# Attention and expert routing on one core: first keys in three parts, late small loads, pad rows spread over SyncE, a new order

## The chip, the core and the metric

One core of a Trainium2 chip runs the whole program. The engines are TensorE (PE), VectorE (DVE), ScalarE (ACT), GpSimd (POOL) and SyncE (SP), which only issues DMAs. Each works through its own instructions strictly in the order in which they stand; engines meet through semaphores. The metric is device microseconds of one launch.

## The reference, cut to what matters

Four batches of attention with pooled keys, then a top-1 mixture of eight experts over all 49,152 rows:

```python
kv_pool = kv.reshape(B, H // r, r, W // r, r, C).mean(axis=(2, 4))   # 4 x 4 means: 768 keys of 128
k = v = kv_pool.reshape(B, -1, C) @ w_sr
s = (q @ k.transpose(0, 2, 1)) / np.sqrt(C)
a = np.exp(s - s.max(-1, keepdims=True)); a /= a.sum(-1, keepdims=True) + 1e-09
x = (a @ v).reshape(B * S, D)                                         # 4 x 12288 rows of 128
logits = unit(x) @ unit(expert_emb).T / tau                           # eight experts
expert_idx = np.argmax(logits, axis=1); gate_w = softmax(logits)[expert_idx]
for e in range(E):
    out[mask] = gate_w[mask, None] * (np.maximum(x[mask] @ w1[e], 0.0) @ w2[e])   # hidden size 1024
```

## The kernel before

**Attention.** The queries are worked through in 96 steps of 512 (24 per batch), each in four tiles of 128 queries by 768 keys. A tile's scores S come from PE, DVE takes the row maxima `nm`, ACT the exponentials `p`. The first `ka` = 16 steps multiply q and K in f32 (`s_mm`, tile `kf`); in the later ones K and V are f16 pairs (a high part and a remainder), and S is a sum of f16 products. For the product with V, `p` is as a rule split into the f16 tiles `phi` and `plo`, turned by DMA transposes, and multiplied in three terms (line 926). In some half steps (two tiles), chosen by the string `em` of the table `X`, `p` stays f32: PE transposes it against `ident` (line 441) and multiplies it with `pw` as it is (line 917). These are called unsplit halves here.

**The head.** Before any score, the keys of the first batch must exist. Twelve loads of 512 KB (`kv_load_0`) bring kv in chunks; DVE adds neighbours in each (lines 501 and 505, tile `kvt`), PE sums rows and turns the chunk with the matrix `window` (line 513), ACT scales six chunks into `pT` (line 564), PE multiplies 384 columns with `w_sr` (line 517), and ACT or DVE copies them to `kf` (lines 578 and 580, letters `kc`). So K comes in two halves. The pooling of batches 1 to 3 is done later in the same way at line 467, on the engine named by the string `kd`.

**Experts.** Rows are sorted by expert through scatters by POOL into `xs_rows` in DRAM, in groups, while attention runs. Then each tile `t` takes 256 rows of one expert (`load`: a transposing DMA, line 1595, and a small one, 1596); 184 whole tiles come first and up to 23 remainder tiles of 128 rows last, with tile 176 the first that has to wait for the last group's scatter. `load_w` copies the expert's 1 MB of f16 weights into one of three buffers `wbuf`, under a condition on a register, since the copy is skipped when the expert stays the same. Row numbers reach SP by register loads (TENSOR_LOAD) from `off_i` and `wi_i`, with checks of their bounds (FUSED_REGOPS and an assert, line 1561). PE computes `ph` (line 1628) and `po` (line 1664). Padding behind each expert's last row is written by eight DMAs of `pad`, and 576 KB of padding rows by `dummies`.

**What sets the order.** Nothing is dispatched at run time. Every operation is put with `add(engine, duration, key, function, *deps)` into a `Plan`; a list scheduler with estimated durations, keys from the table `X` and stand-in delays (`slack`, `dma`) writes the program, so each engine's order is fixed by numbers. DVE and POOL share a port to the local memory; the plan keeps some of their work apart by the flag `port`. Writes into PE's banks go by turns: three tiles `s_tiles` for S, which the head uses too.

Of the kernel before, what the change touches and what calls it, by code (L numbers as in the profile page):

```python
# [44 lines left out]
X = dict(  # L45
    ka=16, da=8.159, di=14.892, db=12.933, dma=1.729, ahead=2.284, av=6.502, av0=1.846, lb=-4.518, l2=3.102, qt=1.955,
    lead=18.786, x=-14.465, r=0.691, s=-1.205, p=14.572, x0=3.032, r0=2.092, s0=1.377, p0=5.813, qt0=-0.263,
    pm="acabacbccabcccabbdacccb", pl="aaaaabaa", nm="AAADA", xn="DAAA", nm0="ADD", xn0="AA", we="ddcdcdaaadcdaccd",
    h=13.707, kv=20.916, kvs=2.272, w0=-14.405, start=23.312, early=21.36, wd=12.952, xw=1.718, qd=21, qs=21.178,
    ql=9.747, em="---------AA-A-A-A-AA-DM-", et=2.859, ec=-0.864, v0=123.118, sd=1, qu=1.461, q0=-66.525, avd=0.626,  # L50
    m=1.052, end=-3.563, ne=-4.766, ge=-0.689, kd="DPD", gk=547.052, wq="AADADDAD", kv1=10.617, kvs1=0.757, tg=-0.003,
    tl=0.397, qe="------------------------", gap=1.8, nb="ADDDD-DAAD-A---DDD-A--D-----DDD--A-D-A-D-DA----D",
    sqm="AASAAAAAAAAAPAAAPSSAPPPS", qm="AAADDDADDAADDADAAADAAAAD", xh="ADPPDADPDAADDAAPAADADADD", nl="-",
    slack={'ACT PE': 0.131, 'ACT DVE': 0.095, 'ACT POOL': -0.009, 'ACT ACT': -0.082, 'DVE PE': 0.32, 'DVE ACT': 0.274, 'DVE POOL': 0.348, 'DVE DVE': 0.013, 'PE ACT': 0.263, 'PE DVE': 0.071, 'PE POOL': -0.1, 'PE SP': -0.11, 'POOL ACT': 0.46015762370487345, 'POOL DVE': 0.111, 'POOL PE': 0.1, 'POOL POOL': 0.07},
    wt=4.0, leadr=22.0, wr=55.0, kf=16, kc="DA", kk=2.199, su=-1.199, vk=-5.844, om="AAAADADA", og=2.027,
# [4 lines left out]
def attention_moe(  # L60
# [71 lines left out]
    rows2 = [cpool.tile([P, GT, RP], F32, name=f"rows{i}") for i in range(2)]  # L132
    ident = cpool.tile([P, P], F32, name="ident")
# [70 lines left out]
    ctx.enter_context(tc.manual_schedule())  # L204
# [34 lines left out]
    class Op:  # L239


        def __init__(self, eng, dur, key, fn, deps, dma, take, free, hold, lands, port, stage):
            self.eng, self.dur, self.key, self.fn, self.dma = eng, dur, key, fn, dma
            self.port = port
            self.take, self.free, self.lands, self.stage = take, free, lands, stage
            self.left, self.users, self.ready, self.end = 0, [], 0.0, None
            if hold:
                self.ready = key + X["start"] - X["early"]
            for d in set(deps):
                if d is not None:  # L250
                    self.left += 1
                    d.users.append(self)

    class Plan:
# [36 lines left out]
        def run(self, begin):  # L291
# [23 lines left out]
            while any(count):  # L315
# [89 lines left out]
                for u in op.users:  # L405
                    if op.dma is not None and u.dma is not None and eng == u.eng and not op.lands:
                        ready = op.end
                    elif op.dma is not None:
                        ready = self.moved + X["dma"]
# [97 lines left out]
    def kv_t_0(i):  # L507
        v = st[0].pop(("kvt", i))
        a, j = divmod(i, NKC // 2)
        st[0]["pp", a] = s_tiles[a]  # L510
        for g in range(KC // R):
            k = (j * (KC // R) + g) * 32
            nc.tensor.matmul(s_tiles[a][:, k : k + 32], v[:, g, 0, :], window, start=True, stop=True)

    def kv_k_0(a):
        st[0]["kp"] = s_tiles[2].rearrange("p (a b) -> p a b", a=2)[:, :, :HB]
        nc.tensor.matmul(
            st[0]["kp"][:, a, :], wsr[:, :C], st[0]["pT"][:, a * HB : (a + 1) * HB], start=True, stop=True
        )

    def kv_max_0(a):
        if a == 0:
# [3 lines left out]
            out=m[:, a : a + 1], in_=st[0]["kp"][:, a, :], axis=AX.X, op=ALU.max, apply_absolute_value=True  # L526
# [33 lines left out]

    def kv_mean(b, a):
# [10 lines left out]
    def kv_k_copy(b, a):  # L572
        if a == 0:
            st[b]["kf"] = kvs.tile([P, NK], F32, tag="kf", name=f"kf{b}")
        if b == 0:
            out, x = st[0]["kf"][:, a * HB : (a + 1) * HB], st[0]["kp"][:, a, :]
            if X["kc"][a] == "A":
                nc.scalar.mul(out, x, SCALE)
            else:
                V.tensor_scalar(out=out, in0=x, scalar1=SCALE, scalar2=None, op0=ALU.mult)  # L580
            return
        nc.scalar.copy(out=st[b]["kf"][:, a * HB : (a + 1) * HB], in_=st[b].pop(("kp", a))[:, :HB])

# [214 lines left out]
    def s_mm(k, j):  # L798
        t = s_tiles[s_turn(k, j)]
        ks[k]["s", j] = t[:, :NK]  # L800
        if unscaled(k):
            for lo, hi in ((0, 512), (512, NK)):
# [737 lines left out]
    def pads():  # L1540
        rows = nc.values_load_multi_w_load_instructions(
            base_i[0:1, :], engines=[nc.sync.engine], min_val=0, max_val=(E - 1) * CAP + NT
        )[1]
        for e in range(E):
            o = nc.s_assert_within(rows[e], e * CAP, e * CAP + NT)
            ins = nc.sync.dma_start(out=xs[ds(o, TR), :].rearrange("(p j) c -> p j c", j=TR // P), in_=pad)
            for key in (*keys, "loads"):
                tc.declare_no_dep(ins.ins, group=key, reason="rows past an expert's last")
            tc.add_to_no_dep_group("loads", ins.ins)
# [6 lines left out]
    def value(name, src, t, top):  # L1556
# [177 lines left out]
    def kv_rows_0():  # L1734
# [3 lines left out]
        for i in range(NKC):  # L1738
            t0, tag = -70.0 + 0.1 * i, kv_tag(i)
            o = took(tag, add("SP", 0.45, t0, lambda i=i: kv_load_0(i), *turn(tag, KV_BUFS[tag]), dma=1.43))  # L1740
# [3 lines left out]
            if i == 3:  # L1744
                x_set = setup(X["su"], x_wsr, x_tau, x_emb, c)
# [5 lines left out]
    def kv_ops(b):  # L1751
# [18 lines left out]
        for a in range(2):  # L1770
            if b == 0:
                key = -60.0 + a
                m = add("ACT", 0.37, key, lambda a=a: kv_mean(b, a), turned[NKC // 2 * (a + 1) - 1], *(turn("pT", 1) if a == 0 else ()))
            else:
                key = t0 + 14.0 + a
                last = mine[(a + 1) * NQR // 2 - 1]
                o = add("PE", 0.64, key, lambda a=a: kv_t(b, a), last, *turn("pT", 1), take=f"pp{b}_{a}")
                reads("pooled", o)
                m = add(
                    "ACT", 0.37, key, lambda a=a: kv_mean(b, a), o, *(turn("pT", 1) if a == 0 else ()),  # L1780
                    free=f"pp{b}_{a}",
                )
# [3 lines left out]
            if b == 0:  # L1786
                o = add("PE", 0.8, key, lambda a=a: kv_k_0(a), m, x_wsr)
                if a == 0:
                    turn("s2", 1), turn("kf", 1)
                    took("s2", o)  # L1790
                else:
                    reads("s2", o)
                reads("pT", o)
                copies.append(add("DVE", 0.5, key + 0.5, lambda a=a: kv_max_0(a), o, *copies))
                on = ENG[X["kc"][a]]
                whole_k.append(add(on, 0.5, key, lambda a=a: kv_k_copy(0, a), o, *whole_k))
                if a == 0:
                    took("kf", whole_k[0])
                reads("s2", copies[-1], whole_k[-1])
                continue  # L1800
# [458 lines left out]
```

## Time and profile before

| | |
|---|---|
| time, three runs | 1948.08, 1948.6, 1950.21 us (median 1948.6) |
| profiled execution | 1957.1 us, of it 1955.4 us span |
| granted TensorE clock | 0.998 |
| PE | 1907.6 us busy, 98% of the span |
| DVE, ACT, POOL | 86%, 75%, 66% |

Busy time counts an engine's instructions, not its waiting. PE's matmuls are pipelined, so a row can begin before the last one ends. The head is the time before the first score, about 27 us; attention runs to about 1770 us with expert tiles woven in, and the rest is the last expert tiles.

### The profile page before, as it was taken

Reading aid. Unit: us, or ns where it says so; the run is one execution under the profiler, and the core shown is the slowest. Engines: PE = TensorE matmul, PEld = TensorE weight load, DVE = VectorE, ACT = ScalarE, POOL = GpSimd, SP = SyncE. Lnnn points to the kernel's source line nnn. Section 1 sums busy time; section 2 is a strip of 40 time slices with the busy share of each in tenths; the row PEclk is TensorE's granted clock in tenths of the full one; section 3 lists DMA queues with packets and bytes.
Section 4 is the critical chain, followed back from the end, with each engine's and each line's share of the span. In section 5 each row is a group of like instructions: output and inputs, shape, how many; then the busy total and the mean of one; then the engine's idle time right before and its main releaser. Section 6 shows DMA issues by size and latency. Waiting matters only on the chain. (4 is left out here: it accounts for less than half of the span.)

```text
span 1955.4 us, 63753 instructions
## 1 busy us (share of the span) xinstructions
PE 1907.6 (98%) x23536; PEld 1677.0 (86%) x23536; DVE 1674.3 (86%) x4037; ACT 1469.7 (75%) x3162; POOL 1292.3 (66%) x1857
## 2 busy tenths in 40 slices
PE   6999999999999999999999999999999999999988
PEld 4787788888888888888888888888888888898988
DVE  7899999988988879888989988988888898886645
ACT  4888877877788778877777877877877788764543
POOL 2547587678886777685676675766766865766544
PEclk9999999999999999999999999999999999999999
DMA  7998889989888999888989899887877777763443
GB/s 256 250 265 206 205 170 175 170 159 172 182 174 169 199 200 177 166 176 153 181 176 170 171 222 177 180 154 144 178 142 161 165 147 145 156 130 67 101 106 122
DMA packets 870923, 333.24 MB, mean 170 GB/s; under 512 B 825794, under 2 KB 836171, under 8 KB 868432
## 3 DMA queue, kind: packets, MB, share of 16 engines
q1 hardware_dynamic: 844624, 274.95, 71.9%
q0 software_dynamic: 24640, 53.53, 9.4%
q8 instruction: 186, 3.05, 0.7%
q14 instruction: 129, 1.06, 0.2%
q10 hardware_dynamic: 1344, 0.66, 0.1%
HBM read 271.41 MB, written 63.19 MB: 171 GB/s over the span
## 5 line engine op out<-in xcount | busy, mean ns | idle before, releaser
L1635 ACT ACTIVATE hh<-ph 128x512 f16<-128x512 f32 x754 | 447.7, 595 | 237.8 <-PE ph L1628 196.0
L1640 DVE SCALAR_TENSOR_TENSOR hl<-ph,hh 128x512 f16<-128x512 f32 x754 | 513.0, 683 | 108.9 <-ACT hh L1635 103.0
L1628 PE MATMUL ph<-x,wbuf 128*128 128x256 f16 x4416 | 594.0, 273 | 11.4 <-DMA wbuf<-w_prep 8.3
L207 POOL DMA_INDIRECT xs_rows<-rows,pi x384 | 442.7, 1153 | 176.6 <-issue 40.0
L207 POOL DMA_INDIRECT out_dram<-o,m x350 | 381.8, 1091 | 227.1 <-ACT o L1684 45.4
L1628 PEld LDWEIGHTS <-wbuf 128*128 128x128 f16 x4848 | 438.7, 98 | 79.1 <-DMA wbuf<-w_prep 12.1
L1664 PE MATMUL po<-wbuf,hh 128*128 128x128 f16 x6032 | 460.3, 219 | 2.9 <-DVE hl L1640 1.1
L1664 PEld LDWEIGHTS <-hh 128*128 128x128 f16 x6176 | 400.5, 98 | 20.7 <-issue 2.6
L810 PE MATMUL s<-k,qT 128*128 128x512 f16 (+1 forms) x1920 | 363.9, 326 | 1.4 <-DVE nm L821 1.4
L821 DVE CUSTOM_DVE_ANT_0 p<-s,scales,qa 128x768 f32<-128x768 f32 x320 | 323.3, 1010 | 41.9 <-PE s L810 38.7
L875 DVE SCALAR_TENSOR_TENSOR plo<-p,phi 128x768 f16<-128x768 f32 x358 | 349.1, 976 | 5.8 <-ACT phi L861 3.5
L840 ACT ACTIVATE p<-p,nm 128x768 f32<-128x768 f32 x320 | 298.8, 934 | 59.2 <-DVE nm L821 56.8
L926 PE MATMUL xp<-v,pthi 128*128 128x136 f16 (+1 forms) x4392 | 319.7, 223 | 1.4 <-ACT pT L564 0.8
L1664 PE MATMUL po<-wbuf,hl 128*128 128x128 f16 x3016 | 291.5, 219 | 0.0
L926 PEld LDWEIGHTS <-pthi 128*128 128x128 f16 x4392 | 278.8, 98 | 14.3 <-issue 2.0
L861 ACT ACTIVATE phi<-p 128x768 f16<-128x768 f32 x310 | 260.8, 843 | 6.6 <-DMA pthi<-phi 3.5
L810 PEld LDWEIGHTS <-qT 128*128 128x128 f16 x1920 | 178.3, 98 | 87.0 <-issue 1.8
L1664 PEld LDWEIGHTS <-hl 128*128 128x128 f16 x3088 | 205.0, 98 | 0.7
L926 PE MATMUL xp<-v,ptlo 128*128 128x136 f16 x2196 | 189.8, 223 | 2.6 <-DMA ptlo<-plo 2.6
L946 ACT ACTIVATE x<-xp,rn 128x135 f32<-128x135 f32 x304 | 96.5, 372 | 77.6 <-DVE rn L938 59.5
L960 POOL TENSOR_TENSOR rows<-x,rows 128x256 f16<-128x256 f32 x192 | 137.4, 720 | 19.1 <-ACT rows L956 14.2
L926 PEld LDWEIGHTS <-ptlo 128*128 128x128 f16 x2196 | 144.0, 98 | 3.0 <-DMA ptlo<-plo 3.0
(416 smaller groups left out, 2045.4 us busy)
## 6 DMA issues: line engine op xcount, KB each, us to landing
wbuf<-w_prep SPq DMA_DIRECT2D x202, 1026.0 KB
q<-in_q_dram SPq DMA_DIRECT2D x48, 512.0 KB
kvt<-in_kv_dram SPq DMA_DIRECT2D x24, 768.0 KB
wf<-in_moe_w_dram SPq DMA_DIRECT2D x16, 512.0 KB
kvt<-in_kv_dram SPq DMA_DIRECT2D x12, 512.0 KB
xs_rows<-rows,pi POOLq DMA_INDIRECT x384
out_dram<-o,m POOLq DMA_INDIRECT x350
w_prep<-wo SPq DMA_DIRECT2D x8, 514.0 KB
```

The costliest lines, as they stand in the source:

```text
L207: ins = nc.gpsimd.indirect_dma_start(out=dst, out_offset=bass.IndirectOffsetOnAxis(ap=idx, axis=0), in_=src, in_offset=None, bounds_check= ...
L810: nc.tensor.matmul(t[:, lo:hi], qs[:, l, :], r[:, lo:hi], start=i == 0, stop=i == 2)
L821: V.tensor_tensor_reduce(out=p, in0=ks[k].pop(("s", j)), in1=scales[:, 4:5].broadcast_to([P, NK]), scale=ks[k]["fac"], scalar=3.0e38, op0= ...
L840: nc.scalar.activation(out=p, in_=s, func=AF.Exp, bias=ks[k].pop(("nm", j)), scale=1.0 if unscaled(k) else -1.0)
L861: nc.scalar.mul(hi, p, PSC)
L875: V.scalar_tensor_tensor(out=lo, in0=ks[k].pop(("p", j)), scalar=PSC, in1=hi, op0=ALU.mult, op1=ALU.subtract)
L926: nc.tensor.matmul(ks[k]["xp", h][:, i, :e], l[:, c, :], r[:, c, :e], start=n == 0, stop=n == len(terms) - 1, skip_group_check=True,)
L960: nc.gpsimd.tensor_tensor(out=r[:, :, C : 2 * C], in0=ks[k]["x"][:, 2 * h : 2 * h + 2, 0:C], in1=r[:, :, 0:C], op=ALU.subtract)
L1628: nc.tensor.matmul(ph[:, kk * n : (kk + 1) * n], weights(t, o + f, P), r, start=i == 0, stop=i == 2)
L1635: nc.scalar.activation(out=hh, in_=ts[t]["ph", u], func=AF.Relu)
L1640: V.scalar_tensor_tensor(out=hl, in0=ts[t].pop(("ph", u)), scalar=0.0, in1=ts[t]["hh", u], op0=ALU.max, op1=ALU.subtract)
L1664: nc.tensor.matmul(ts[t]["po"][:, j * C : (j + 1) * C], h[:, kk * n + j * P : kk * n + (j + 1) * P], weights(t, f, P), start=u == 0 and i ...
```

## The change

**K in three parts.** The chunks 6 to 11 go to another bank, and `kv_mean_0`, `kv_k_0` and `kv_k_copy_0` run over the columns 0 to 384, 384 to 640 and 640 to 768. The first two tiles of S are split, so that their first 512 columns need only the first two parts.

```diff
+    KP = ((0, HB), (HB, NK - X["kt"] * 64), (NK - X["kt"] * 64, NK))
+    def kv_k_0(n):
+        a, (lo, hi) = min(n, 1), KP[n]
+        if n < 2:
+            st[0]["kp", a] = s_tiles[1][:, :HB] if a == 0 else s_tiles[2][:, 512 : 512 + HB]
         nc.tensor.matmul(
-            st[0]["kp"][:, a, :], wsr[:, :C], st[0]["pT"][:, a * HB : (a + 1) * HB], start=True, stop=True
+            st[0]["kp", a][:, lo - a * HB : hi - a * HB], wsr[:, :C], st[0]["pT"][:, lo:hi], start=True, stop=True
         )
...
+            if k == 0 and j < X["sh"]:
+                o = add("PE", 0.86, key, lambda j=j: s_mm(k, j, 0), hi, lo, *whole_k[:2], *turn(tag, 1))
+                uses["kf"][0].append(o)
+                o = add("PE", 0.43, key, lambda j=j: s_mm(k, j, 1), o, *deps)
```

**Small loads and constants.** The load of `tau` (one number to 128 partitions) and the padding rows of `dummies` move from about 0 and 33 us to later places. The constants are written before the plan's own work on their engines, and the chain that normalises `emb` (`setup`) follows the last chunk, not the fourth.

```diff
+    ctx.enter_context(tc.manual_schedule())
     ident = cpool.tile([P, P], F32, name="ident")
...
-    x_tau = add("ACT", 0.1, -60.0, lambda: nc.scalar.dma_start(out=tau_b, in_=tau.broadcast_to([P, 1])), dma=0.06)
+    x_tau = add("ACT", 0.3, X["tau"], lambda: nc.scalar.dma_start(out=tau_b, in_=tau.broadcast_to([P, 1])), dma=0.3, hold=True)
...
-    x_dummies = add("ACT", 0.1, 30.0, dummies, dma=3.1, hold=True)
+    x_dummies = add("ACT", 0.1, TS[NSTEP - 10], dummies, dma=4.2, hold=True)
...
-            if i == 3:
-                x_set = setup(X["su"], x_wsr, x_tau, x_emb, c)
+            if i == NKC - 1:
+                x_set = setup(X["su"], x_wsr, x_emb, c)
```

**Padding on SP, and checks.** The eight writes of `pad` become eight operations, each with its own register load, put 4 us apart in the plan. The register loads of the last tiles leave their bounds checks out.

```diff
-    def pads():
-        rows = nc.values_load_multi_w_load_instructions(
-            base_i[0:1, :], engines=[nc.sync.engine], min_val=0, max_val=(E - 1) * CAP + NT
-        )[1]
-        for e in range(E):
-            o = nc.s_assert_within(rows[e], e * CAP, e * CAP + NT)
...
+    def pads(e):
+        o = nc.sync.value_load(base_i[0:1, e : e + 1], min_val=e * CAP, max_val=e * CAP + NT)
...
-                src[0:1, i : min(i + 4, NTILE)], engines=[nc.sync.engine], min_val=0, max_val=top
+                src[0:1, i : min(i + 4, NTILE)], engines=[nc.sync.engine], min_val=0, max_val=top,
+                skip_runtime_bounds_check_because="the rows and weights of a tile are bounded where they are worked out",
```

**The table.** Most numbers and strings of `X` are new. Two lines of many:

```diff
-    ql=9.747, em="---------AA-A-A-A-AA-DM-", et=2.859, ec=-0.864, v0=123.118, sd=1, qu=1.461, q0=-66.525, avd=0.626,
-    m=1.052, end=-3.563, ne=-4.766, ge=-0.689, kd="DPD", gk=547.052, wq="AADADDAD", kv1=10.617, kvs1=0.757, tg=-0.003,
+    xw=1.718, qd=21, qs=19.803, ql=10.318, em="---A-----MA-D-M-A-AA-DM-", et=3.494, ec=0.254, v0=104.065, sd=1,
+    qu=-0.424, q0=-65.932, avd=-0.301, m=-0.039, end=-3.551, ne=-6.905, ge=-1.176, kd="DPP", gk=228.829,
```

In the program as written this makes 120 transposes of `p` on PE and 120 unsplit products with V in place of 108 each, 24 and 12 fewer split products of the two kinds at line 926, 182 pairs of DMA transposes in place of 183, and 16 pooling adds of each size on POOL in place of 8, since batch 3 is pooled there and not on DVE.

On PE, the head. Before: the columns of the last two chunks (`kvt` 10 and 11) into the bank s_159, the transposes of q, `emb` and `wsr`, the second half of K into s_160, and the first S tile.

```order
L513 MATMUL s_159<-window,kvt_10_232 128x32 x2
L513 MATMUL s_159<-window,kvt_11_242 128x32 x2
L441 MATMUL pq_285<-ident,q_251 128x128 x4
L441 MATMUL pe<-ident,emb_sb 128x8
L441 MATMUL pe<-ident,wsr 128x128
L517 MATMUL s_160<-pT_238,wsr 128x384
L1275 MATMUL pe<-wt 128x7
L803 MATMUL s_158<-kf_255,qT_294 128x512
```

The same place in the change:

```order
L515 MATMUL s_160<-window,kvt_10_221 128x32 x2
L523 MATMUL s_160<-pT_233,wsr 128x256
L515 MATMUL s_160<-window,kvt_11_227 128x32 x2
L443 MATMUL pq_274<-ident,q_235 128x128 x4
L523 MATMUL s_160<-pT_233,wsr 128x128
L818 MATMUL s_158<-kf_245,qT_286 128x512
L543 MATMUL bound<-m_250,ones_97 128x1 x2
L818 MATMUL s_158<-kf_245,qT_286 128x256
```

Behind the last chunk stand now a product of 128 columns and no work of `setup`; the first 512 columns of S stand ahead of the 256 others, with the product `bound` between.

On SP, near the end of attention. Before: the register loads, weight copies and the eight writes of `pad` (the rows between repeat the check and the write).

```order
L1571 DMA wbuf_2878<-w_prep 128x4104
L1541 TENSOR_LOAD base_i
L1541 ISA x16
L1545 REGISTER_ALU
L1545 ISA
L1546 ISA
L1546 DMA xs_rows<-pad 128x144
```

The same place in the change:

```order
L1583 DMA wbuf_2799<-w_prep 128x4104
L1556 TENSOR_LOAD base_i
L1556 ISA x2
L1557 ISA
L1557 DMA xs_rows<-pad 128x144
L1569 TENSOR_LOAD off_i
L1569 ISA x2
L1607 ISA
L1607 DMA_TRANSPOSE x_40967<-xs_rows 128x2x256
L1608 ISA
L1608 DMA ml<-xs_rows 128x2x2
L1556 TENSOR_LOAD base_i
```

One `pad` write stands there now between a weight copy and the load of a tile, and the other seven are spread in the same way from tile 170 to tile 176.

## Rows read from the trace of the kernel before

**Rows 1.** The page: busy time of each engine, share of the span, instructions.

```profile
PE 1907.6 (98%) x23536; PEld 1677.0 (86%) x23536; DVE 1674.3 (86%) x4037; ACT 1469.7 (75%) x3162; POOL 1292.3 (66%) x1857
```

**Rows 2.** Busy time by stage: us, PE, PEld, DVE, ACT, POOL, PEclk, DMA share, GB/s.

```profile
600.00:800.00 200.00, 196.03 (x2484) 172.92 (x2481) 174.63 (x421) 158.36 (x342) 149.44 (x218) 1.00 0.96 191
...
1000.00:1200.00 200.00, 195.34 (x2500) 172.81 (x2499) 178.55 (x427) 156.33 (x344) 134.02 (x195) 1.00 0.95 188
```

**Rows 3.** DMA queues between 5 and 7 us: packets, MB, share of 16 engines.

```profile
q1 hardware_dynamic: 66, 0.20, 28.3%
q10 hardware_dynamic: 133, 0.00, 3.5%
```

**Rows 4.** Timeline of the head: start, us, engine, line, operation, idle before.

```profile
4.66 0.69 DVE L501 TENSOR_TENSOR kvt<-kvt 128x512 f32<-128x512 f32 x1 [3.20 <-DMA kvt<-in_kv_dram]
...
8.95 0.69 DVE L501 TENSOR_TENSOR kvt<-kvt 128x512 f32<-128x512 f32 x1 [1.92 <-DMA kvt<-in_kv_dram]
...
18.09 0.56 DVE L580 TENSOR_SCALAR kf<-s 128x384 f32<-128x384 f32 x1 [0.54 <-PE s L517]
...
21.80 0.43 DVE L505 TENSOR_TENSOR kvt<-kvt 128x256 f32<-128x256 f32 x1
...
24.65 1.49 PE L517 MATMUL s<-pT,wsr 128*128 128x384 f32 x2
...
29.73 0.96 DVE L814 TENSOR_REDUCE nm<-s 128x1 f32<-128x768 f32 x1 [2.27 <-PE s L803]
```

**Rows 5.** Waits of PE between 36 and 50 us: total, times, longest.

```profile
PE w_m L658 <- DVE w_t L653: 3.7, 1, 3.7
```

**Rows 6.** Lines 1541 and 1561 on SP: duration min/median/max ns, first to last start.

```profile
L1541 SPq FUSED_REGOPS  x8: 147/147/164, 1791.1 to 1792.8; - x8
...
L1541 SPq TENSOR_LOAD <-base_i x1: 544/544/544, 1790.5 to 1790.5; - x1
...
L1561 SPq FUSED_REGOPS  x56: 147/154/176, 1834.0 to 1937.5; - x56
```

**Rows 7.** Timeline of SP in the last stage: start, us, operation.

```profile
1793.41 6.96 SPq L1546 DMA_DIRECT2D xs_rows<-pad  x8
...
1845.22 1.25 SPq L1595 DMA_TRANSPOSE x<-xs_rows  x1
...
1873.04 0.08 SPq L1571 DMA_DIRECT2D wbuf<-w_prep  x1
```

**Rows 8.** Timeline of PE in the last stage, idle time in brackets.

```profile
1804.77 1.46 PE L1628 MATMUL ph<-x,wbuf 128*128 128x256 f16 x6 [2.56 <-DMA wbuf<-w_prep]
...
1808.84 0.82 PE L1628 MATMUL ph<-x,wbuf 128*128 128x256 f16 x6
...
1810.17 0.82 PE L1628 MATMUL ph<-x,wbuf 128*128 128x256 f16 x6
...
1873.15 1.48 PE L1628 MATMUL ph<-x,wbuf 128*128 128x256 f16 x12 [2.27 <-DMA wbuf<-w_prep]
```

**Rows 9.** Busy time by stage (columns of group 2) around the first stall.

```profile
1804.00:1808.00 4.00, 3.23 (x23) 2.71 (x24) 1.78 (x5) 0.60 (x1) 1.77 (x4) 0.57 0.46 56
```

**Rows 10.** Waits after 1700 us: total, times, longest.

```profile
PE ph L1628 <- DMA wbuf<-w_prep: 8.2, 8, 2.6
```

**Rows 11.** Groups by line, all of the span: busy us, mean ns.

```profile
L441 PE MATMUL s<-ident,p 128*128 128x128 f32 x108 | 14.0, 274 | 0.1
...
L917 PE MATMUL xp<-v,pw 128*128 128x136 f32 x216 | 26.8, 280 | 0.0
```

**Rows 12.** Timeline of PE at the first two split tiles of attention.

```profile
56.37 0.87 PE L926 MATMUL xp<-v,pthi 128*128 128x136 f16 x12 [0.17 <-DVE v L624]
...
57.43 0.87 PE L926 MATMUL xp<-v,pthi 128*128 128x136 f16 x12
```

**Rows 13.** Waits of SP between 1845 and 1915 us: total, times, longest.

```profile
SPq L1595 <- DMA xs_rows<-rows,pi: 5.0, 1, 5.0
```

**Rows 14.** Line 467, pooling adds of batches 1 to 3, on POOL: ns.

```profile
L467 POOL TENSOR_TENSOR kvt<-kvt x24: 723/1275/2377, 440.6 to 755.4; 96x1024 f32<-96x1024 f32 x8, 96x512 f32<-96x512 f32 x8, 96x256 f32<-96x256 f32 x8
```

More of the change, by code (lines that the diff above doesn't have):

```diff
@@ L245, in __init__ @@
             self.take, self.free, self.lands, self.stage = take, free, lands, stage
-            self.left, self.users, self.ready, self.end = 0, [], 0.0, None
+            self.left, self.users, self.ready, self.end, self.quick = 0, [], 0.0, None, False
             if hold:
@@ L801, in s_mm @@
         if unscaled(k):
-            for lo, hi in ((0, 512), (512, NK)):
+            for lo, hi in ((0, 512), (512, NK))[slice(part, None if part is None else part + 1)]:
                 nc.tensor.matmul(
@@ L1538, in pad_rows @@
         V.tensor_copy(out=base_i, in_=total)
-    def pads():
-        rows = nc.values_load_multi_w_load_instructions(
-            base_i[0:1, :], engines=[nc.sync.engine], min_val=0, max_val=(E - 1) * CAP + NT
-        )[1]
-        for e in range(E):
-            o = nc.s_assert_within(rows[e], e * CAP, e * CAP + NT)
[L1546 to L1549, printed above, removed]
+    def pads(e):
+        o = nc.sync.value_load(base_i[0:1, e : e + 1], min_val=e * CAP, max_val=e * CAP + NT)
+        ins = nc.sync.dma_start(out=xs[ds(o, TR), :].rearrange("(p j) c -> p j c", j=TR // P), in_=pad)
+        for key in (*keys, "loads"):
+            tc.declare_no_dep(ins.ins, group=key, reason="rows past an expert's last")
+        tc.add_to_no_dep_group("loads", ins.ins)
     def size(t):
@@ L1769, in kv_ops @@
         turned = kv_rows_0() if b == 0 else None
[L1770 to L1773, printed above, removed]
-            else:
[L1775 to L1782, printed above, removed]
+        parts, key = [], X["k0"] + 1
+        for n in range(0 if b else 3):
+            lo, hi = KP[n]
+            key = X["k0"] + n
+            w = (hi - lo) / HB
+            m = add("ACT", 0.15 + 0.22 * w, key, lambda n=n: kv_mean_0(n), turned[hi // 64 - 1], *(turn("pT", 1) if n == 0 else ()))
+            if n == 0:
+                took("pT", m)
+            if n != 1:
+                means.append(m)
+            o = add("PE", 0.1 + 0.6 * w, key, lambda n=n: kv_k_0(n), m, x_wsr)
+            reads("pT", o)
+            tag = f"s{min(n, 1) + 1}"
+            if n < 2:
+                turn(tag, 1), took(tag, o)
+            else:
+                reads(tag, o)
+            if n == 0:
+                turn("kf", 1)
+            parts.append(o)
+            if n != 1:
+                copies.append(add("DVE", 0.5, key + X["km"], lambda a=n // 2: kv_max_0(a), *parts[n // 2 :], *copies))
+                reads(tag, copies[-1])
+            on = ENG[X["kc"][n]]
+            whole_k.append(add(on, 0.15 + 0.27 * w, key, lambda n=n: kv_k_copy_0(n), o, *whole_k))
+            if n == 0:
+                took("kf", whole_k[0])
+            reads(tag, whole_k[-1])
+        for a in range(2 if b else 0):
+            key = t0 + 14.0 + a
+            last = mine[(a + 1) * NQR // 2 - 1]
+            o = add("PE", 0.64, key, lambda a=a: kv_t(b, a), last, *turn("pT", 1), take=f"pp{b}_{a}")
+            reads("pooled", o)
+            m = add(
+                "ACT", 0.37, key, lambda a=a: kv_mean(b, a), o, *(turn("pT", 1) if a == 0 else ()),
+                free=f"pp{b}_{a}",
+            )
             if a == 0:
@@ L2148, in attention_moe @@
     o = add("DVE", 0.1, t + 1.0, lambda: pad_rows(base[NGRP % 3]), end)
-    x_pads = add("SP", 4.0, t + 2.0, pads, o, dma=1.0, lands=True)
+    x_pads = []
+    for e in range(E):
+        x_pads.append(add("SP", 0.95, t + 2.0 + X["pd"] * e, lambda e=e: pads(e), o, *x_pads[-1:], dma=0.1, lands=True))
     rest = chain(t + 10.0, 0.3, remainder(base[NGRP % 3]), end, chosen[NSEL - 1][-1], dur=0.12)
@@ L2169, in attention_moe @@
             turn(tx, 1), turn(tm, 1)
-        ld = add("SP", 2.5 if t < NA - PER else 1.9, s - (X["lead"] if whole else X["leadr"]), lambda t=t: load(t), *deps, *(turn(tx, XB) if whole else ()), *turn(tm, OB + 2 if t < NA - ML else NTILE), dma=1.3 * size(t) / Q)
+        ld = add("SP", 2.5 if t < NA - PER else 1.5 if t % 4 else 2.5, s - (X["lead"] if whole else X["leadr"]), lambda t=t: load(t), *deps, *(turn(tx, XB) if whole else ()), *turn(tm, OB + 2 if t < NA - ML else NTILE), dma=1.3 * size(t) / Q)
         took(tx, ld)
```

79 lines of the change are left out of this document (36 added, 43 removed).

## The prediction

> **What bounds the kernel now.** I read the page's line of busy times first. PE is busy for 1907.6 us [rows 1] of a span of 1955.4, so its work alone holds 98% and all the time that it idles is 47.8 us. The reader is to see two things in that: what adds work to PE costs in full, and what removes a wait can win 47.8 us at most. The busy times by stage say where the idle time lies. In the bulk of attention there is little: 3.97 us between 600 and 800 [rows 2], 4.66 between 1000 and 1200. The rest is at the two ends, so I read those as timelines, and their waits.
>
> *The head.* DVE's first add starts at 4.66, its last ends at 22.23 (21.80 and 0.43), K's second half runs on PE at 24.65, and the first row maximum `nm` at 29.73 [rows 4]. Twelve chunks of two adds (0.69 and 0.43, about 1.2 with the steps between) would take DVE 14.4 us; it took 17.6. The DMA view explains a part: between 5 and 7 us the kv queue q1 used only 28.3% of the engines, while q10, with 133 packets of almost no bytes, used 3.5% [rows 3]. These are mostly `tau`, one number sent to 128 partitions.
>
> *Attention's first 100 us.* The one large wait of PE is for `w_t`, once, 3.7 us [rows 5].
>
> *The tail.* SP loads a register from `base_i` at 1790.5, checks it eight times (1791.1 to 1792.8, so 0.24 us each) [rows 6], and then needs 6.96 us from 1793.41 for the eight `pad` writes [rows 7]. So it is held from 1790.5 to 1800.4, and the weight copy queued behind comes late: PE idles 2.56 us until 1804.77 [rows 8]. It goes on at a lower clock: the mean granted clock from 1804 to 1808 is 0.57 of 2.4 GHz [rows 9]. One round of `ph` and `po` takes 1.33 us later (1808.84 to 1810.17), the two rounds after the stall took 4.07, so 1.4 us went there. In all PE waits 8 times for `wbuf` after 1700, 8.2 us [rows 10]. The largest of the others shows who is late: SP issues a (conditional) copy at 1873.04 [rows 7], and PE starts at 1873.15 after 2.27 us of waiting [rows 8]. A megabyte does not move in 0.11 us, so this copy was skipped, and PE waited for SP's instructions.
>
> **The change, part by part.** The sum is made on the profiled execution (1957.1 us), which lies 8.5 above the median of the three runs; I take the same difference off the median.
>
> *K earlier, first part: DVE.* With the constants ahead of the first chunk (they fit into the time before 4.66, where DVE waits for data) and the `emb` chain behind the last, DVE's chain is 4.66 + 12 x 1.2 + two operations on K's first half of 0.56 (`kf` at 18.09 [rows 4] and its maximum, taken as equal) = 20.2 instead of 22.23: **-2.0**. This needs the hole at 5 to 7 us to go with `tau`. If it stays, DVE starts the third chunk at 8.95 as now, after 1.92 us of waiting [rows 4], and 8.95 + 10 x 1.2 + 1.1 = 22.05: -0.2. The Trainium skill, "DMA: Bandwidth & Descriptors", section "Queues, rings and completion order", says that each DMA engine takes turns between its queues, packet by packet. By that, 133 tiny packets should cost kv hardly more than their own 3.5%, and the hole would be someone else's; the trace shows kv starved in just those 2 us, but not by whom. I take the trace's coincidence, with the other case as a rival.
>
> *K earlier, second part: from the last columns to the first maximum,* 7.5 us now. The last product has 128 columns in place of 384, so a third of 1.49 us [rows 4]: -1.0. Its copy is shorter by about 0.3, and the first 512 columns of S run ahead without it; of that I count 0.6, since the 256 others still wait for the third part. **-1.9** (bounds 0 and -3). The setup's three small products go from a place where PE waits to one where it works: three at about 0.2 (a 128x128 transpose costs 0.27 [rows 11]), **+0.6**.
>
> *The 3.7 us wait for `w_t`.* The same ACT and POOL work on the weights stands around it in the new order, so **0**. Were it to vanish it would be -3.7.
>
> *One more unsplit half step.* Two tiles. The 108 transposes now are 18 tiles: 14.0/18 = 0.78 us a tile, the products 26.8/18 = 1.49 [rows 11]. A split tile costs 1.06 (56.37 to 57.43 [rows 12]). 2 x (0.78 + 1.49 - 1.06) = **+2.4**, in full, since PE is the bound.
>
> *Pads spread.* Ahead of the copy that came late stand three writes in place of eight. The stall of 2.56 and its 1.4 at a lower clock go: **-4.0** (bounds 0 and -4.0). SP pays for it: eight loads of 0.54 in place of one [rows 6], with eight checks and 6.96 us of writes 13.2 us in place of 9.9, 3.3 more before tile 176. What hides this is a wait: SP stands still for 5.0 us for the last scatter into `xs_rows` [rows 13] before it loads that tile at 1845.22 [rows 7]. If the scatter comes earlier that cover shrinks, and up to 3 us come back.
>
> *Checks left out.* 56 checks between 1834.0 and 1937.5 [rows 6] at 0.24 are 13.4 us of SP. The later waits for `wbuf` are 8.2 - 2.56 = 5.6 us; those of SP's kind, like the one at 1873, go, while copies that really move a megabyte still take their time. I take a little over half, **-3.0** (0 to -5.6).
>
> *`dummies` later.* 576 KB at the 190 GB/s that the bulk moves [rows 2] are 3 us of the queues; no wait of PE is put down to it now. **0**, and +3 if loads that PE needs stand behind it.
>
> *Everything else in the table* moves work between DVE, ACT and POOL, none onto PE: **0**, within 4 either way, the idle time of one 200 us stretch [rows 2].
>
> Sum: -2.0 - 1.9 + 0.6 + 2.4 - 4.0 - 3.0 = -7.9. The profiled execution would take 1949.2, the median **1940.7 us**. A measurement of this kernel tells about 0.2%, 3.9 us, from no change.
>
> **The rivals.**
>
> *A, the forecast.* Chance 0.45.
>
> *B, the head's lead is lost.* Either the hole isn't `tau`'s (the -2.0 shrinks to -0.2: 1942.5), or the first steps of attention, where PE waits for ACT and DVE and not the other way, eat all 3.9 us: 1944.6. For it: the wait for `w_t` [rows 5] shows that PE isn't the bound there. Against: an earlier start also moves ACT's and DVE's first work forward. Chance 0.18.
>
> *C, the tail's relief is eaten.* SP spends 3.3 us more ahead of tile 176, and if the copies for the remainder stay late, the -3.0 go, and up to 3 of the stall come back: 1943.7 to 1946.7. For it: PE arrives there some 7 us earlier (stall and checks), while the scatters are set by POOL. Against: the 5.0 us of SP's wait [rows 13]. Chance 0.16.
>
> *D, slower.* Batch 3 is now pooled by POOL: 32 adds, 24 of which took 1.275 us (median) on POOL for batch 2 [rows 14]. DVE shares its port with POOL; a DVE operation that meets one is held for up to that long. DVE is the engine next to PE in attention (178.55 of 200 us between 1000 and 1200 [rows 2]). If ten of the 32 hit an operation on which PE waits, 12.8 us come on top and the kernel is slower than before by 5: 1953; seven give 1949.6, no change. Against: batch 2, pooled by POOL, lies in a stretch with 3.97 us of idle PE, batch 3, by DVE, in one with 4.66. Chance 0.08.
>
> *E, better.* The bulk's gaps shrink too, or the 3.7 us at `w_t` go: 1937, and down to 1933 with the 4 us of the table's term. Nothing in the profile promises it beyond the four us or so of idle PE in each such stretch [rows 2]. Chance 0.13.
>
> **How the numbers follow.** The likeliest is A, 1940.7, with its own range 1937 to 1944. B and C lie above it, E below. 1932 to 1948 leaves out D, the far end of E and a little of the rest, 0.15 to 0.2 in all. Faster by over 0.2% means below 1944.7: A and E, most of B and half of C, 0.76. Within 0.2%: the rest of B and C and a part of D, 0.16. Slower: D beyond seven held adds, and mishaps of the new order, 0.08.
>
> **What would show it.** In the profile of the changed kernel: no hole in kv's queue at 5 to 7 us, DVE's last column add ending near 20.2, the first `nm` near 25.8; PE's wait for `w_t` still there; no wait for `wbuf` around 1800 and no low clock behind it; the waits after 1850 for `wbuf` down to about 2.5 us; PE busy for about 2 us more than 1907.6 (2.4 + 0.6, less the part of the 1.4 at the lower clock); SP's wait before tile 176 shorter. The prediction is wrong if PE idles more than before between 1000 and 1200 (D), if the first `nm` stays at 29 (B), or if PE waits for the load of tile 176 (C).

## The result and the profile after

The changed kernel takes 1974.22 us (median of six runs, 1970.29 to 1978.61), the kernel before 1951.06 beside it: 1.0115 of it, 95% interval 1.0099 to 1.013. It is slower by some 23 us, where 8 us faster were forecast.

The page's line of busy times of the changed kernel answers to [rows 1]; its span is 1973.3 us.

```profile
PE 1917.5 (97%) x23538; PEld 1684.4 (85%) x23538; DVE 1718.8 (87%) x4083; ACT 1444.4 (73%) x3040; POOL 1328.4 (67%) x1894
```

PE is busy for 9.9 us more, and idle for 1973.3 - 1917.5 = 55.8 us, 8.0 more than before. The mean granted clock is 0.994 in place of 0.998; as lost time that is at most 0.006 x 1973.3 = 11.8 us against 3.9. But PE was busy for only 17.5 of the 23.6 us recorded at the lower level (1.2 GHz in place of 2.4), and before for 6.4 of 7.7, so by an estimate half of these, 8.7 and 3.2 us, were lost: 5.5 more. The other 4.4 of the 9.9 are about the 2.4 forecast for the unsplit half step, and more time at half speed in the head (below). Of the 17.9 us between the two spans 8.0 are thus idle time and some 5.5 low clock, and little is work.

Where they arise is shown by the *lag*: the start of the first S product of each step (lines 803 and 810 before, 818 and 825 after, taken one by one from the traces, from the span's first instruction) minus that of the same step in the kernel before. "Tile 183" is the first `ph` of the last whole expert tile. The expectations below state lags of the changed kernel 0.5 us lower, since they count from another origin.

| lag in us at | step 0 | 5 | 12 | 24 | 36 | 48 | 60 | 66 | 72 | 94 | tile 183 | end |
|---|---|---|---|---|---|---|---|---|---|---|---|---|
| changed kernel | -2.5 | 6.5 | 10.8 | 11.6 | 16.4 | 20.5 | 25.2 | 34.8 | 29.4 | 30.3 | 20.6 | 17.9 |
| the same, changed_again | -2.5 | 6.6 | 8.0 | 9.3 | 14.1 | 21.6 | 20.1 | 31.6 | 26.0 | 26.8 | 17.1 | 14.5 |

The head wins 2.5 us and the tail 12 (30.3 to 17.9). Between them attention loses 33, in all batches but the last. The second row is the same program in a later run (`changed_again`, below): it loses 29, and at a single step two traces of one program differ by up to 5 us, so a smaller difference between two traces of attention says little.

*The head.* The timeline of the changed kernel, columns as in [rows 4]:

```profile
4.74 0.69 DVE L503 TENSOR_TENSOR kvt<-kvt 128x512 f32<-128x512 f32 x1 [0.32 <-DMA kvt<-in_kv_dram]
...
20.18 0.42 DVE L507 TENSOR_TENSOR kvt<-kvt 128x256 f32<-128x256 f32 x1
...
21.14 1.22 PE L523 MATMUL s<-pT,wsr 128*128 128x256 f32 x2 [0.47 <-ACT pT L571]
...
22.15 0.90 PE L515 MATMUL s<-window,kvt 128*128 128x32 f32 x4
...
23.75 0.74 PE L523 MATMUL s<-pT,wsr 128*128 128x128 f32 x2
...
24.63 2.07 PE L818 MATMUL s<-kf,qT 128*128 128x512 f32 x2
...
26.50 0.85 PE L543 MATMUL bound<-m,ones 128*128 128x1 f32 x4
...
27.21 2.05 PE L818 MATMUL s<-kf,qT 128*128 128x256 f32 x3
...
28.45 0.96 DVE L829 TENSOR_REDUCE nm<-s 128x1 f32<-128x768 f32 x1 [0.72 <-PE s L818]
```

And in the kernel before:

```profile
22.28 0.93 PEld L513 LDWEIGHTS s<-window,kvt 128*128 128x128 f32 x4 [0.20 <-DVE es L1255]
...
27.10 2.59 PE L803 MATMUL s<-kf,qT 128*128 128x512 f32 x4
...
32.69 1.46 PE L803 MATMUL s<-kf,qT 128*128 128x512 f32 x4
```

DVE's last add ends at 20.60 (forecast 20.2, before 22.23), and the last product of K is short. But two things stand in the way in PE's order. The product of K's middle 256 columns (line 523, 21.14) stands ahead of the last chunk's columns (line 515), so these begin at 22.15, 1.55 us after the last add; before they began at 22.28, 0.05 us after it. And the second half of the first S tile, 256 columns, stands at 27.21 behind `bound` (line 543, 26.50), which costs 0.7. So the first `nm` comes at 28.45, 1.3 us earlier than before and not 3.9. PE is also slower in the head: a tile of S takes 2.59 us at 27.10 and 1.46 at 32.69 in the kernel before. By such lengths PE ran at the lower level until about 29.4 us there, and until about 31.5 in the changed kernel; the trace's records of the granted clock begin only then. The hole in kv's queue between 5 and 7 us is gone; q1 in the DMA view, as in [rows 3]:

```profile
q1 hardware_dynamic: 208, 0.74, 92.8%
```

*The tail.* In the busy times by stage PE hardly idles any more:

```profile
1800.00:1850.00 50.00, 50.00 (x684) 47.44 (x682) 34.79 (x96) 27.93 (x57) 34.43 (x57) 1.00 0.34 74
1850.00:1900.00 50.00, 50.00 (x684) 47.45 (x682) 29.95 (x63) 28.31 (x56) 26.93 (x29) 1.00 0.48 110
```

*Attention.* The two stretches of [rows 2]:

```profile
600.00:800.00 200.00, 192.41 (x2403) 168.96 (x2401) 179.77 (x424) 149.70 (x322) 152.05 (x209) 0.99 0.96 183
1000.00:1200.00 200.00, 188.93 (x2329) 164.74 (x2327) 181.46 (x399) 145.59 (x307) 154.83 (x211) 0.97 0.92 186
```

Idle time went from 3.97 to 7.59 us and from 4.66 to 11.07, and the second has a granted clock of 0.97. Over all of attention the changed kernel has this row:

```profile
25.00:1800.00 1775.00, 1734.14 (x21005) 1510.38 (x21005) 1597.22 (x3810) 1354.04 (x2866) 1231.88 (x1750) 0.99 0.86 172
```

And the kernel before, in its own stretch of attention:

```profile
28.00:1770.00 1742.00, 1719.20 (x20979) 1500.18 (x20978) 1551.79 (x3745) 1379.37 (x2989) 1193.28 (x1709) 1.00 0.87 175
```

PE idles for 40.9 us where it idled for 22.8. Its largest waits there in the changed kernel (total, times, longest):

```profile
PE v_m L443 <- DVE m L700: 4.9, 1, 4.9
PE xp L941 <- DMA ptlo<-plo: 4.8, 4, 2.3
PE po L1676 <- DVE hl L1652: 4.7, 5, 2.1
PE s L818 <- ACT p L855: 4.1, 5, 1.7
PE ph L1640 <- DVE hl L1652: 4.0, 3, 1.7
PE w_m L673 <- DVE w_t L668: 2.6, 3, 1.7
```

And in the kernel before:

```profile
PE w_m L658 <- DVE w_t L653: 3.7, 1, 3.7
PE xp L926 <- DMA ptlo<-plo: 2.6, 2, 2.0
PE ph L1628 <- DMA wbuf<-w_prep: 2.4, 1, 2.4
PE s L803 <- ACT p L840: 1.9, 5, 1.0
PE ph L1628 <- DVE hl L1640: 1.7, 2, 1.5
```

No one wait makes up the difference. Most are waits for DVE, 27 us in all where it was 12, and the largest shows how such a loss comes about. The timeline of the changed kernel around 1175 us:

```profile
1172.62 0.35 SPq L1583 DMA_DIRECT2D wbuf<-w_prep  x1
...
1179.13 0.23 DVE L1687 TENSOR_SCALAR m<-m,wbuf 128x2 f32<-128x2 f32 x1 [4.64 <-DMA wbuf<-w_prep]
1179.27 0.95 DVE L890 SCALAR_TENSOR_TENSOR plo<-p,phi 128x768 f16<-128x768 f32 x1
...
1180.13 0.95 DVE L700 TENSOR_REDUCE m<-kf 128x1 f32<-128x768 f32 x1
...
1181.23 0.37 PE L443 MATMUL v_m<-ident,m 128*1 128x128 f32 x1 [4.94 <-DVE m L700]
```

The busy times over the stretch that follows:

```profile
1175.00:1190.00 15.00, 10.06 (x97) 7.96 (x96) 9.64 (x27) 5.79 (x12) 7.52 (x13) 0.77 0.93 244
```

A copy of new weights is issued at 1172.62. DVE's next operation is a small one (line 1687) that needs these weights, and waits 4.64 us for them. Behind it stand `plo` and the maximum of the next batch's keys (line 700), and for that PE waits 4.94 us. What follows on PE runs at a lower clock (0.77 in the mean over the 15 us, where the two levels are 1.2 and 2.4 GHz), so the wait costs more than its own 4.94 us. Between steps 64 and 66, where it lies, the lag grows by 8.9 us, and by 10.3 in `changed_again`.

### The profile page after: what moved, and what is told of

Same layout as the page of the kernel before. It is cut to its first block, busy times and chain, and to the rows that moved or that the text cites. A ratio compares the mean times of both kernels' runs of the same rounds, so it can differ in the third digit from the quotient of the medians.

```text
span 1973.3 us, 63520 instructions
## 1 busy us (share of the span) xinstructions
PE 1917.5 (97%) x23538; PEld 1684.4 (85%) x23538; DVE 1718.8 (87%) x4083; ACT 1444.4 (73%) x3040; POOL 1328.4 (67%) x1894
## 5 line engine op out<-in xcount | busy, mean ns | idle before, releaser
L209 POOL DMA_INDIRECT xs_rows<-rows,pi x384 | 437.2, 1138 | 176.5 <-issue 36.9
L890 DVE SCALAR_TENSOR_TENSOR plo<-p,phi 128x768 f16<-128x768 f32 x357 | 354.3, 993 | 0.9 <-ACT phi L876 0.6
L975 POOL TENSOR_TENSOR rows<-x,rows 128x256 f16<-128x256 f32 x192 | 138.5, 725 | 18.2 <-ACT rows L971 13.9
L992 ACT ACTIVATE junk<-x 128x128 bf16<-128x128 f32 x376 | 113.6, 308 | 26.1 <-DVE x L963 25.8
```

The costliest lines, as they stand in the source:

```text
L209: ins = nc.gpsimd.indirect_dma_start(out=dst, out_offset=bass.IndirectOffsetOnAxis(ap=idx, axis=0), in_=src, in_offset=None, bounds_check= ...
L890: V.scalar_tensor_tensor(out=lo, in0=ks[k].pop(("p", j)), scalar=PSC, in1=hi, op0=ALU.mult, op1=ALU.subtract)
L975: nc.gpsimd.tensor_tensor(out=r[:, :, C : 2 * C], in0=ks[k]["x"][:, 2 * h : 2 * h + 2, 0:C], in1=r[:, :, 0:C], op=ALU.subtract)
```

## The experiments

**First, table and written code apart, and two suspects.** `table_only` is the kernel before with the new `X`, `written_only` the changed code with the old `X` (and new numbers only for what the old one lacks):

```diff
 X = dict(   # table_only, in the kernel before
-    ka=16, da=8.159, di=14.892, db=12.933, dma=1.729, ahead=2.284, ...
+    ka=16, da=8.159, di=14.892, db=13.957, dma=1.729, ahead=3.713, ...
 X = dict(   # written_only, in the changed kernel
-    ka=16, da=8.159, di=14.892, db=13.957, dma=1.729, ahead=3.713, ...
+    ka=16, da=8.159, di=14.892, db=12.933, dma=1.729, ahead=2.284, ...
# pool3_on_dve, in the changed kernel
-    kd="DPP"
+    kd="DPD"
# tau_late, in the kernel before
-    x_tau = add("ACT", 0.1, -60.0, ...
+    x_tau = add("ACT", 0.3, 21.127, ..., dma=0.3, hold=True)
```

> The kernel before with nothing changed but the table X (all numbers and strings of the changed kernel that it knows). Theory 1, the table's new order of attention is what costs: against the kernel before the changed one is 3 us ahead at the first score, 10 us behind by step 15, 30 us behind by step 66, and gains 10 us back in the tail, so the table alone, without the head's and the tail's gain, should give 1951 + 25 to 33 = 1976 to 1984 us. Theory 2, the written changes (late tau, constants, pads, three parts of K) cost and the table is harmless: within 5 us of 1951.

> The changed kernel's code with the old table (and the new numbers only for what the old table lacks: the parts of K, the late tau, the distance of the pads). Theory 1: the head's 3 to 4 us and the tail's 7 to 10 us stay, the losses in attention go: 1951 - 10 = 1938 to 1944 us. Theory 2: 1965 to 1975 us.

> The changed kernel with one letter back: batch 3 pooled by DVE (kd = DPD). If the pooling on POOL is what costs at steps 57 to 72 (the lag grows there from 19.5 to 28.9 us): about 9 us faster than the changed kernel, 1965 us. If the order around it does, whoever pools: within 4 us of 1974.

> The kernel before with only the load of tau moved behind the first chunks' work. If tau makes the hole in the kv queue at 5 to 7 us: no hole, DVE's last column add about 1 to 2 us earlier than 22.23, and 1949 to 1950 us in all. If not: the hole is still there and the last add ends at 22.2.

| kernel | median us | ratio to before | 95% interval |
|---|---|---|---|
| table_only | 1976.65 | 1.0108 | 1.0084 to 1.0132 |
| written_only | 1972.12 | 1.0098 | 1.0075 to 1.012 |
| pool3_on_dve | 1968.13 | 1.0077 | 1.0054 to 1.01 |
| tau_late | 1952.04 | 0.9995 | 0.998 to 1.001 |

Both theories fall in this form: the table alone loses, and so does the code alone with the old table. What they have in common is that either rewrites attention's order. Batch 3 on DVE gives back 5 to 6 us (1968.1 after 1974.2 and, in `changed_again`, 1972.9; the kernels were not run beside each other, and the intervals of their ratios overlap). That the pooling on POOL is the cause is not shown: between steps 57 and 72 the lag grows by 3.5 with batch 3 on DVE and by 9.0 in the changed kernel, but by only 4.7 in `changed_again`, the same program, and by 8.6 in `written_only`, where DVE pools batch 3. `tau` is what made the hole; q1 in `tau_late` between 5 and 7 us:

```profile
q1 hardware_dynamic: 208, 0.75, 95.3%
```

The last add ends there at 21.25, 1.0 us earlier, and the time is the same. The rule of the Trainium skill that I had weighed ("DMA: Bandwidth & Descriptors", section "Queues, rings and completion order": engines take turns between queues by packets) does not account for this alone: with the load of 128 small pieces both queues together used 31.8% of the engines (28.3% and 3.5% [rows 3]), and without it q1 used 95.3%.

**Second, the parts that keep the order, and another order of the same work.** `tail_only` and `kept_order` have the old table and these parts of the change; attention's rows stand as in the kernel before. `reorder_only` changes one number, `three_parts_tail` keeps K in three parts and the tail.

```diff
# tail_only: the eight pads(e), skip_runtime_bounds_check_because=...
-    x_pads = add("SP", 4.0, t + 2.0, pads, o, dma=1.0, lands=True)
+        x_pads.append(add("SP", 0.95, t + 2.0 + 4.0 * e, lambda e=e: pads(e), ...))
# kept_order: tail_only, tau_late, and
+    ctx.enter_context(tc.manual_schedule())
     ident = cpool.tile([P, P], F32, name="ident")
# reorder_only, in the kernel before
-    da=8.159
+    da=8.17
```

> The kernel before with the old table and only the two changes of the tail: the eight pad writes spread on SP, each with its own register load, and the bounds checks of the last tiles left out. All of attention keeps its order row by row. If the tail's two terms of the prediction hold (4.0 and 3.0 us): 1952 - 7 = 1945 us, no wait for wbuf near 1800 and less than 3 us of them later. If they only move the stall to the load of tile 176: within 3 us of 1952.

> The kernel before with the old table and every written part of the change that leaves attention's order as it was: the tail's two, tau late, the constants first. If the parts are good and only the new order is bad: 1952 - 7 - 2 to 3 = 1942 to 1943 us, faster than both kernels, with the lag against the kernel before constant from step 1 to step 94. If late tau or the constants cost something in attention: 1945 or more.

> The kernel before with one number of its table changed by 0.13% (da from 8.159 to 8.17): no operation more or less, the same pooling engines and unsplit half steps, but the list scheduler writes another order for all of attention (8560 lines of difference on PE). Theory 1a, the order before fits the chip by chance or search and any other loses: 1965 to 1975 us, with the lag growing in the first 20 steps and at the changes of batch, and more idle time and low clock on PE. Theory 1b, the new table's own choices (one more unsplit half step, pooling on POOL, other engines) are what costs: within 5 us of 1952.

> The changed kernel's code with the old table, and tau, the constants, the emb chain and the padding rows back at their old places: K in three parts and the tail's two changes stay. The order of attention is another than before (6649 lines on PE). Theory 1a: the head gains 2 us, the tail 7, attention loses 10 to 25, so 1953 to 1968 us. If late tau, the constants or the padding rows caused the loss that the changed code shows with the old table: 1943 us.

| kernel | median us | ratio to before | 95% interval |
|---|---|---|---|
| tail_only | 1944.43 | 0.9951 | 0.9932 to 0.9969 |
| kept_order | 1945.15 | 0.9952 | 0.9934 to 0.997 |
| reorder_only | 1966.12 | 1.0059 | 1.0038 to 1.008 |
| three_parts_tail | 1953.57 | 0.9994 | 0.998 to 1.0008 |

The tail holds its 7 us and more: `tail_only` is some 10 us faster than the kernel before (0.5%, 0.3 to 0.7), and so faster than both kernels. A `pad` write by itself takes SP 0.39 us; the first of them in SP's timeline:

```profile
1789.51 0.39 SPq L1542 DMA_DIRECT2D xs_rows<-pad  x1
```

With its register load, which starts at 1788.76, that is 1.14 us, so 9.1 for eight. Of PE's waits for `wbuf` after 1700 one is left:

```profile
PE ph L1625 <- DMA wbuf<-w_prep: 0.3, 1, 0.3
```

The early parts of `kept_order` add nothing that can be measured; 2 to 3 us were expected. `three_parts_tail` came out at the low end of what was expected for another order: with the tail's gain it takes the time of the kernel before. And a change of one number by 0.13%, with no operation more or less, costs 0.6%. Its busy times over attention:

```profile
28.00:1780.00 1752.00, 1720.68 (x20945) 1499.47 (x20944) 1553.53 (x3744) 1379.67 (x2988) 1182.73 (x1707) 1.00 0.87 174
```

PE's work in it is the same as before (1720.68 against 1719.20 us) and its idle time is 31.3 us against 22.8.

`written_only` and `three_parts_tail` ran on one chip, both with the old table, K in three parts and the tail. They differ in `tau`, the constants, the chain of `setup`, the padding rows and the plan's estimate for the first loads, and in the order that these give; the time differs by 18.6 us. `tau` and the constants cost nothing in `kept_order`. No run moves the padding rows alone: in `written_only` they go out at 1193.93, where its lag jumps by 9.7 us (steps 64 to 66), so there they may cost something. In the changed kernel they go out at 1209.57, behind the jump, and the lag falls from there (34.8 to 29.4).

**Third, the weight copies, and two more orders.** At two places where the lag grows, near 680 to 720 and 1155 to 1190 us, three copies of new weights are issued.

```diff
# after_no_copies, before_no_copies
-        nc.sync.dma_start(..., cond=w < E * P)
+        nc.sync.dma_start(..., cond=w < E * P if t < WB or t >= NA - ML else w + 1 < 1)
# after_reorder, in the changed kernel: da=8.18; reorder_2, in the kernel before: da=8.15
```

> The changed kernel with the copies of new weights left out between tile 3 and tile 165 (their condition is never true there), so most tiles are computed with the wrong expert's weights; every instruction stands where it stood. Between 680 and 720 us and between 1155 and 1190 us three such copies of a megabyte are issued on SP, and there the lag against the kernel before grows (from 11.5 us at step 33 to 20.0 at step 48, from 19.9 at step 57 to 28.9 at step 72). If the copies, by what they delay in this order, are what costs there: 12 to 17 us faster than the changed kernel, 1957 to 1962 us. If the work on the next batch's keys and values does: within 4 us of 1974.

> The same copies left out of the kernel before, wrong weights too. In its trace PE waits 2.4 us for one of them and some 3 us more around them. If its order stands the copies well: 1947 to 1950 us, so the lag of the changed kernel without copies against this one stays flat from step 33 to 94. If both kernels pay alike for them: both get faster by the same 10 us or more.

> The changed kernel with one number of its table changed by 0.26% (da from 8.159 to 8.18), which makes another order of the same work (6924 lines of difference on PE). If the order of the changed kernel is one of many that fit the chip alike: within 12 us of 1974, on either side. If the searched order is a good one for the chip, as that of before was: 10 us slower or more, 1984.

> The kernel before with da at 8.15 in place of 8.159, again another order of the same work (8664 lines on PE). If the first reordering's 10 us are what leaving the old order costs: 1962 to 1972 us. If that was one bad order: within 5 us of 1952.

| kernel | median us | ratio to before | 95% interval |
|---|---|---|---|
| after_no_copies | 1967.14 | 1.0058 | 1.0038 to 1.0078 |
| before_no_copies | 1942.9 | 0.9936 | 0.9916 to 0.9956 |
| after_reorder | 1974.93 | 1.0104 | 1.0072 to 1.0137 |
| reorder_2 | 1965.97 | 1.0066 | 1.0045 to 1.0087 |

My theory of the copies falls as the cause of the difference. They cost the kernel before 11 us and the changed one 7 by the medians and 9 to 11 by the ratios (it did not run beside); without them the two lie 24 us apart, as with them. The stall at 1175 us is real: without the copies the lag grows by 2.7 us between steps 64 and 66, not by 8.9. But the kernel before pays for its copies too, in part at other places. The two reorderings of the kernel before agree: each costs 10 to 13 us. The changed kernel's own order is no such point: one other order of its work takes the same time.

| lag in us at | step 0 | 5 | 12 | 24 | 36 | 48 | 60 | 66 | 72 | 94 | tile 183 | end |
|---|---|---|---|---|---|---|---|---|---|---|---|---|
| reorder_only | 0.0 | 0.3 | 2.5 | 3.1 | 8.2 | 13.0 | 11.8 | 10.8 | 12.5 | 12.3 | 9.5 | 9.0 |
| reorder_2 | 0.1 | 0.1 | 3.8 | 2.2 | 8.4 | 10.5 | 8.5 | 8.4 | 11.0 | 10.6 | 8.8 | 5.9 |
| written_only | -2.3 | 3.7 | 5.3 | 12.8 | 14.3 | 18.3 | 17.3 | 27.2 | 26.6 | 25.8 | 17.4 | 14.5 |
| three_parts_tail | -0.3 | 7.6 | 15.3 | 17.9 | 18.2 | 18.5 | 16.2 | 13.7 | 11.3 | 12.2 | 4.1 | 1.3 |
| table_only | 0.0 | 7.2 | 8.9 | 16.4 | 24.1 | 26.0 | 23.6 | 31.4 | 25.8 | 24.9 | 18.1 | 20.0 |
| after_reorder | -2.5 | 4.8 | 6.5 | 7.8 | 15.2 | 17.4 | 17.0 | 33.6 | 27.6 | 27.5 | 17.8 | 15.7 |
| tail_only | -0.2 | -0.8 | -0.8 | -2.5 | -2.3 | -1.1 | -2.5 | -2.1 | -2.1 | -1.7 | -9.6 | -12.5 |

**Fourth, letters against numbers of the new table.** Still open was why attention loses 33 us and not 11. `letters_old` is the changed kernel with the old table's strings but `kc`, `letters_new` the kernel before with the new ones, `em_old` the changed kernel with the old `em`.

```diff
# em_old, in the changed kernel
-    em="---A-----MA-D-M-A-AA-DM-"
+    em="---------AA-A-A-A-AA-DM-"
```

> The changed kernel with the letters of the old table (which engine does what, which half steps stay unsplit, batch 3 pooled by DVE) and the new numbers (keys, delays). Theory L, the new letters are what costs beyond the 11 us of leaving the old order (more work on DVE, batch 3 on POOL, one more unsplit half step): 1956 to 1964 us. Theory N, the new numbers are: 1970 to 1976 us.

> The kernel before with the letters of the new table (except kc, the copy of K) and its old numbers. Theory L: 1966, the time of a reordering, and 8 to 15 us more: 1974 to 1981 us. Theory N: 1964 to 1968 us, as after any reordering.

> The changed kernel with the old string em, so without the half step in the second step of the first batch that is no longer split. The 2.4 us of PE work that it adds by the prediction go, and the order changes with it: 1968 to 1974 us if it only costs PE that; 1962 or less if an unsplit half step so early is what makes the first batch's lag grow by 14 us (from -3 at the first score to 11 at step 24).

They took 2036.62 us (1.0098, 1.0072 to 1.0124), 2053.74 (1.0164, 1.0135 to 1.0194) and 2051.8 (1.0169, 1.0145 to 1.0193), on a chip on which the kernel before took 2018.47. So the changed kernel was run beside the first two again, on another chip:

> The changed kernel itself, on the same chip as the two runs beside it, since the chip of the last three runs took 2018 us for the kernel before and cannot be set against the earlier ones. 1.010 to 1.013 of the kernel before.

> The changed kernel with the old table's letters and its new numbers, once more beside the changed kernel. Theory L: 10 us or more faster than the changed kernel beside it. Theory N: within 5 us of it.

> The kernel before with the new table's letters and its old numbers, once more. Theory L: a ratio of 1.011 to 1.016 to the kernel before, more than the 1.006 and 1.007 of the two reorderings. Theory N: 1.004 to 1.008.

| kernel | median us | ratio to before | 95% interval |
|---|---|---|---|
| changed_again | 1972.89 | 1.0103 | 1.0087 to 1.012 |
| letters_old_again | 1976.22 | 1.0117 | 1.01 to 1.0134 |
| letters_new_again | 1978.79 | 1.0129 | 1.0112 to 1.0146 |

By `letters_old_again` theory L falls: with the old letters and the new numbers the time is that of the changed kernel. By `letters_new_again` theory N falls too: the new letters with the old numbers lose more than a reordering does. Either half of the new table, joined to the other half of the old one, loses as much as the whole. `em_old` stays inconclusive, since the changed kernel did not run beside it.

## Why the prediction was wrong

**The step that failed** is the last term of the sum: "*Everything else in the table* moves work between DVE, ACT and POOL, none onto PE: **0**, within 4 either way". The lag says +33 us (from -2.5 to 30.3; 29 in `changed_again`). I had read the little idle time that the bulk showed before as a property of the work, when it belonged to this one order of it. The reorderings show it: the same work in another order idles 8.5 us more in attention and is 10 to 13 us slower. The mean granted clock moved little there (0.997 and 0.995 after 0.998; 0.994 in the changed kernel). Nor does the term end with the table: the written changes with the old table lose 28 us in attention too (`written_only`, from -2.3 to 25.8), and no term of the sum priced the order that they bring.

**What is shown of the 33 us and what is not.** Some 11 are what leaving the old order costs, if the two reorderings stand for the new order (12.3 and 10.6 at step 94). Batch 3 on POOL may be worth 5 to 6, measured with the order changing along with it. The unsplit half step is 2.4 by the prediction's arithmetic; no run settles it. The rest, 13 us by these figures, was not settled, and that the pieces add up is itself not shown: the new table with the old code, the old table with the new code, and each half of the table joined to the other's all lie at 1.010 to 1.013. The largest piece, 14 us, is lost in the first batch (the changed kernel goes from -2.5 to 11.6 by step 24, and `three_parts_tail` and `table_only` are 16 to 18 us behind there), where the wait for `w_t` [rows 5] had shown that PE waits for others.

**Head.** First part right: -1.6 for -2.0, by DVE's last add, and the hole was `tau`'s. Second part wrong: -1.9 forecast, none came; from the last column add to `nm` it takes 7.85 us now and 7.5 before. The last chunk's columns stand behind the product of 256 columns (1.5 us), and the 256 columns of S behind `bound` (0.7). I had shown that order and not priced it. Rival B had the place, and less than the price: the 2.5 us at the first S are gone by step 1, where the lag is 2.0, and it grows from there. About half of the 4.5 us from -2.5 to 2.0 is the clock, by an estimate: from its first S product PE ran for 6.8 us at the lower level, and before for 2.3, and half of the difference is 2.3 us.

**Tail.** Right in kind and too small: the stall and the low clock near 1800 are gone, and so are the waits after 1850. Forecast were 7.0 us; in `tail_only` the lag falls by 7.9 from step 94 to tile 183 and by 10.8 to the end. The mis-sized term is that of the checks: nearly all of the 5.6 us of later waits went, where I had counted 3.0. What the pads and the checks give singly no run shows. The 3.3 us that I had charged to SP did not come: eight writes with their loads take 9.1 us of SP and not 13.2, since a load of one number takes 0.28 and not 0.54. So rival C fell.

**The wait for `w_t`** stayed in other shape: 2.6 us for it in attention, with 4.1 for ACT's `p` beside it.

**Rival D** had the right sign, and its mark came: PE idles for 11.07 us between 1000 and 1200, where it idled for 4.66. But the largest wait there is the one at 1175 us, for a copy of weights, and the lag jumps at the same steps in `written_only`, where DVE pools batch 3; its mechanism is not shown. The way to lose that came, another order, had only the words "mishaps of the new order" and a part of the 0.08.

## What to carry to other kernels

Where a program's order is fixed by numbers, rewriting the order is itself a term of the sum, and its price can be measured before anything else: change one number by a part in a thousand and time it. In two such tries here that costs 10 to 13 us, more than all the edits together were to win. Parts of a change that leave the order alone can be taken by themselves: the tail's two edits on the old table are faster than both kernels.

## What the runs showed of the hardware

A load of one number to 128 partitions held another queue's large transfers back for 2 us: between 5 and 7 us q1 used 28.3% of the engines with it and 95.3% without it (`tau_late`). And chips differ: on one of them the kernel before took 2018.47 us (2006.66 to 2022.31) in place of 1951 to 1956, and PE had waits for nothing that the profile shows. In the profile's groups of `letters_old` there (busy, mean ns, idle before and its releasers), 12.4 us of such waits stand before `po` alone:

```profile
L1746 PE MATMUL po<-wbuf,hh 128*128 128x128 f16 x6032 | 464.0, 219 | 18.3 <-issue 12.4 <-ACT hh L1717 2.6 <-ACT o L1766 1.7
```

The same program in `letters_old_again`, on another chip:

```profile
L1746 PE MATMUL po<-wbuf,hh 128*128 128x128 f16 x6032 | 460.1, 219 | 0.3
```
